# Constants built at the start, the last product on another engine, and the first expert's search work in another order, in an attention and two-layer expert kernel

## The chip, the cores and the metric

One core of a Trainium2 chip. The time is the device time of one launch, in microseconds (us); the kernel before has a median of 1419.82 us over three runs (1418.33 to 1420.47). The engines are TensorE (PE; its weight loads are listed as PEld), VectorE (DVE), ScalarE (ACT), GpSimd (POOL) and SyncE (SP, which only issues transfers here).

## The reference

Three stages, each fed by the one before.

```python
# attention with 32 state rows for each of 8 batches and 8 heads (S=512, D=64)
a  = softmax(x @ state.T / 8);  xread = a @ state
a2 = softmax(state @ x.T / 8);  sread = a2 @ x
x  = concat([xread, sread])                    # 4608 tokens x 512
# experts with a room of 576 tokens each: logits sorted over all (token, expert) pairs
for idx in argsort(-(x @ w_gate).flatten()):
    if token is free and expert has room: assign
for e in range(8): out[mask_e] = relu(x[mask_e] @ w1[e]) @ w2[e]
# gated layer on all tokens
out = (silu(out @ w_gate2) * (out @ w_val)) @ w_out
```

The assignment is a greedy walk through 36,864 sorted pairs. The kernel gets the same result by closing one expert after another: it finds which expert fills up first, at which threshold, gives that expert its tokens, and repeats.

## The kernel before, in words

**Attention** runs over the batches in a loop `for b in range(B + 1)`. A string names the order of the steps of one turn (`ORDER` for the middle turns, `HEAD` and `TAIL` for the first and the last): `z` the scores, `m` and `e` one softmax (`center`, `exps1`), `f` the other (`exps2`), `t` and `x` transposes, `r` and `s` the two products with the values (`xread`, `sread`), `p` and `q` the preparation of the next batch's state. Turn b finishes batch b-1 and starts batch b. `xread` leaves an undivided product `xu`; DVE takes the reciprocals `rd` of the sums, forms the router's logits (`xw`, summed into `Lw`), and POOL multiplies `xu` by `rd` into `xm`, which is stored in DRAM as `xm_d`. Step `c` builds constants for the search: in turn 1 the table `IE` on POOL, in turn 5 the rest of POOL's, in turn 6 those of DVE (lines 650 to 718). Step `k` in turn 7 makes the keys of the first 24 of 34 token columns and counts them (`keys`, `count128`, `digits`).

**The search** (`search`, `place`, `close`) works on one expert at a time. `keys` (lines 414 to 432) turns the best remaining logit of each token into an integer key and its digits. `count128` compares the top digit with 128 levels (tile `I`, DVE) and counts by matmuls with `G` (PE). Five more rounds refine the threshold: compare (`I`, DVE), count (PE), copy `ev`, sum (PE), `fe`, spread (PE), `jb`. `place` makes the list `idx` of the expert's token rows. `close` takes the expert out of the logits (`Lw`, line 595) and counts how much room every expert has left (`ca`, `cr`, `crb`, a matmul, `need`; lines 597 to 606).

**The experts** are 8 times 16 units: `hidden` makes 128 hidden columns for half of an expert's tokens (12 matmuls, tile `h`), `expert_out` multiplies them by the second weights (12 matmuls, tiles `y`). Weights and activations are split into an upper part (ACT) and a lower part (DVE: `lo[k]`, line 1014; `w`, lines 756 and 995; `xl`, line 813; `hl`, line 833). Tokens are fetched by `gather` (POOL, from `xm_d` by `idx`) and transposed by `turn` (PE into `bt`, ACT `xh`, DVE `xl`). A table `P_` says at which unit each load, gather, transpose and search is written: `lead` and `hook` for the search, `l0` and `lp` for 16 loads of 64-bit weights of the last layer, which are converted 6 units later. While the units of expert 0 run, the search for expert 1 runs between them on PE and DVE, since expert 1's tokens are not known before.

A list scheduler orders the instructions of each engine; each engine then runs its list in that order. `tc.issue_after(ins)` puts what follows behind `ins` on that instruction's own engine. What stands behind a waiting instruction on the same engine waits too.

After the experts the last layer fills PE with matmuls (line 1106) to the end.

Of the kernel before, what the change touches and what calls it, by code (L numbers as in the profile page):

```python
# [35 lines left out]
E = 8  # L36
# [9 lines left out]
P_ = {'spin': 20, 'xl': 2, 'pc': (0, 9), 'ct': 12, 'cuts': (0, 34), 'lead': [0, 1, 10, 25, 44, 57, 73, 89], 'hook': ['p', 'i', 'p', 'p', 'p', 'x', 'p', 'p'], 'w': [8, 14, 8, 8, 8, 8, 8, 8], 'whook': 'h', 'g': [0, 3, 18, 36, 56, 70, 85, 103], 'gs': 0.34, 't': [0, 14, 29, 46, 61, 75, 91, 104], 'ts': 1, 'ghook': 'p', 'thook': None, 't0': (2, 4, 5), 'l0': 10, 'lp': 6.2, 'cd': 6, 'lhook': 'hh', 'chook': 'h', 'swap': [], 'y0': 16, 'f0': [10, 4, 3]}  # L46
PRE = 24
HEAD = "z0 m0 f0 p l z1 m1 x0 x3 x2 e0 f1 x1 e1 q"
ORDER = "z0 f0 p t0 t1 z1 G l m0 f1 x0 m1 r0 x1 s0 e0 r1 x2 x3 r2 s1 k e1 c q r3"
# [8 lines left out]
def moe_kernel(ctx: ExitStack, tc: tile.TileContext, x, state, moe_w_gate, moe_w1, moe_w2,  # L58
# [57 lines left out]
    def load_state(b0, b1):  # L116
        for g in range(2):
            nc.scalar.dma_start(S2[:, b0:b1, g, 0, :],
                                state[b0:b1, 4 * g:4 * g + 4].rearrange("b h n d -> (h n) b d"))
        nc.gpsimd.tensor_copy(S2[:, b0:b1, :, 1, :], S2[:, b0:b1, :, 0, :])  # L120
        nc.gpsimd.tensor_copy(SC[:, b0:b1, :, :D], S2[:, b0:b1, :, 0, :])
# [19 lines left out]
    load_x(0)  # L141
    wg4 = ac.tile([64, H, E], F32, name="wg4")
# [83 lines left out]
    def turn_x(b, r):  # L226
# [6 lines left out]
        if True:  # L233
# [6 lines left out]
            nc.vector.tensor_tensor(xl[:, :, r, :], v, f32(xh[:, :, r, :]), OP.subtract)  # L240
# [66 lines left out]
    def xread(b, r):  # L307
# [10 lines left out]
        for g in range(2):  # L318
# [6 lines left out]
            nc.scalar.copy(xu[:, r % 2, 4 * g:4 * g + 4].rearrange("p h c -> p (h c)"), px)  # L325
        if r % 2:
# [9 lines left out]
            if b < B - 1 or r == 1:  # L336
                rm = aw.tile([128, 2, H], F32, name="rm", bufs=2)
                nc.vector.tensor_copy(rm, rd)
                rd = rm

            def values(rd=rd):
                hooks["m"] = nc.gpsimd.tensor_tensor(xm[:, q], xu[:, :, :, :D],
                                                     rd[:, :, :, None].to_broadcast([128, 2, H, D]), OP.mult).ins
# [3 lines left out]
            if b < B - 1 or r == 1:  # L347
                values()
            else:
                late.append((values, rd))  # L350
# [51 lines left out]
    def keys(c0, c1, first):  # L402
# [13 lines left out]
        if not first:  # L416
# [5 lines left out]
        nc.vector.tensor_tensor(t8, t8, w8b, OP.mult)  # L422
        sh, bits = DIGITS[0]
        nc.vector.tensor_scalar(dgi[:, 0], key, sh, (1 << bits) - 1,
                                op0=OP.logical_shift_right, op1=OP.bitwise_and)
        nc.vector.tensor_reduce(am, t8, AX.X, OP.max)
# [33 lines left out]
    def search(i, psum, partial=None):  # L460
        pieces = ((0, 6), (6, 9)) if i == 0 else tuple(zip(P_["pc"], P_["pc"][1:]))
# [42 lines left out]
    def place(i, psum, found):  # L504
# [63 lines left out]
        cuts = [0, 8, 16, 24, NC] if i == 0 else P_["cuts"]  # L568
# [12 lines left out]
    def close(i, psum):  # L581
# [13 lines left out]
        nc.vector.tensor_tensor(Lw, Lw, dn[:, None, :].to_broadcast([128, NC, E]), OP.add)  # L595
# [4 lines left out]
        hooks["cr"] = nc.vector.tensor_reduce(cr, ca.rearrange("p c e -> p e c"), AX.X, OP.add).ins  # L600
# [8 lines left out]
    IE = sel.tile([128, 129, 4], BF, name="IE")  # L609

# [4 lines left out]
    prep_gate(0)  # L615

    for b in range(B + 1):
        steps = ORDER if 0 < b < B else HEAD if b == 0 else TAIL
        for op in steps.split():
# [27 lines left out]
            elif k == "c":  # L647
                if b == 1:
                    with tc.issue_after(hooks["m"]):
                        nc.gpsimd.iota(IE, pattern=[[1, 129], [0, 4]], base=0, channel_multiplier=0,  # L650
                                       allow_small_or_imprecise_dtypes=True)
                elif b == 5:
                    with tc.issue_after(hooks["m"]):
                        I32i = ac.tile([128, 32, 4], BF, name="I32i")
                        nc.gpsimd.iota(I32i, pattern=[[1, 32], [0, 4]], base=1, channel_multiplier=0,
                                       allow_small_or_imprecise_dtypes=True)
                        units = sel.tile([128, 6], F32, name="units")
                        unit = sel.tile([128, 6, 128], BF, name="unit")
                        for s in range(6):
                            nc.gpsimd.memset(units[:, s:s + 1], 2.0 ** (-6 * s))  # L660
                            nc.gpsimd.memset(unit[:, s, :], 2.0 ** (-6 * s - (2 if s else 0)))

                        SL_i = ac.tile([128, 4, 4, 32], F32, name="SL_i")
                        nc.gpsimd.iota(SL_i, pattern=[[1, 4], [0, 4], [4, 32]], base=0, channel_multiplier=-1,
                                       allow_small_or_imprecise_dtypes=True)
                        onesf = ac.tile([128, 128], F32, name="onesf")
                        nc.gpsimd.memset(onesf, 1.0)
                        trif = ac.tile([128, 128], F32, name="trif")
                        nc.gpsimd.affine_select(trif, onesf, pattern=[[1, 128]], compare_op=OP.is_gt, fill=0.0,
                                                base=0, channel_multiplier=-1)  # L670
                        minus1 = sel.tile([128, 128], BF, name="minus1")
                        nc.gpsimd.memset(minus1, -2.0 ** -7)
                        ones2 = sel.tile([128, 2], BF, name="ones2")
# [724 lines left out]
```

## Time and profile before

| | |
|---|---|
| median of 3 runs | 1419.82 us |
| the profiled execution | 1420.64 us |
| its span, first to last instruction | 1418.1 us |
| PE busy | 1357.2 us, 96% |
| DVE busy | 1053.9 us, 74% |
| ACT busy | 571.7 us, 40% |
| POOL busy | 441.8 us, 31% |
| mean granted clock of TensorE | 0.98 |

The shares are means over stages that differ. Attention lasts to about 146 us, the first search to 171.6 us, the eight experts to about 620 us, and the last layer from there to the end. In the last two PE is the busy engine; ahead of them DVE is.

### The profile page before, as it was taken

The page shows a single profiled execution, that of the slowest core. Times are in us where ns is not written, and L with a number is a line of the kernel's source. Part 1 is how long each engine was busy: PE and PEld are TensorE (multiplying, and loading weights), DVE is VectorE, ACT ScalarE, POOL GpSimd, SP SyncE. Part 2 cuts the span into 40 slices and gives each one's busy share as a digit, 9 for nine tenths or more (in the row PEclk, how much of TensorE's full clock was granted, in tenths as well). Part 3 has the DMA queues.
Part 4 walks back from the last instruction along what each step waited for, and adds up shares of the span by engine and source line. Part 5 has one row for each costly group of instructions (what it writes and reads, how often), then busy time and mean ns, then how long its engine had stood idle before and what let it go on. Part 6 is the DMA issues. An engine that isn't in the chain of part 4 may idle for free.

```text
span 1418.1 us, 28991 instructions
## 1 busy us (share of the span) xinstructions
PE 1357.2 (96%) x11449; PEld 1318.0 (93%) x11449; DVE 1053.9 (74%) x2067; ACT 571.7 (40%) x1124; POOL 441.8 (31%) x388
## 2 busy tenths in 40 slices
PE   6998489999999999999999999999999999999996
PEld 5876288999999999999999999999999999999996
DVE  5879778886987664559767677776667788998872
ACT  6885123333333343434324335332333464444440
POOL 5766201010201010434213210012211108788871
PEclk9999599999999999999999999999999999999999
DMA  7542325543454454437547466455675784344431
GB/s 135 131 117 82 119 75 195 179 152 123 158 176 151 145 190 144 144 126 263 179 149 248 177 230 235 153 201 193 243 270 208 260 305 149 120 147 151 150 104 45
DMA packets 123335, 238.36 MB, mean 168 GB/s; under 512 B 47808, under 2 KB 57024, under 8 KB 116800
## 3 DMA queue, kind: packets, MB, share of 16 engines
q1 hardware_dynamic: 110096, 209.75, 43.8%
q0 software_dynamic: 5536, 17.83, 3.7%
q10 hardware_dynamic: 7568, 8.95, 2.1%
q8 instruction: 89, 1.46, 0.4%
q14 instruction: 46, 0.38, 0.1%
HBM read 153.65 MB, written 82.84 MB: 167 GB/s over the span
## 4 chain that ended last, share of the span: by engine, by line
PE 81%; DVE 6%; issue 5%; ACT 3%; DMA 2%; POOL 1%; ACTq 0%; POOLq 0%; SPq 0%; DVEq 0%
PE b L1106 50%; PE h L828 13%; PE y L847 4%; PE y L843 4%; PE y L844 4%; PE bt L807 1%; PE pt L236 1%; PE ps L363 1%; PE acc L483 1%; ACT xu L325 1%; ACT RBh L220 1%; DVE yb L872 1%; DMA xg<-xm_d,idx 1%; DMA raw<-y_d 0%; ACT zb L288 0%
## 5 line engine op out<-in xcount | busy, mean ns | idle before, releaser
L1106 PE MATMUL b<-yb,w 128*128 128x256 f32 x4320 | 516.2, 282 | 3.4 <-DVE cs L1156 2.5
L1106 PEld LDWEIGHTS b<-yb,w 128*128 128x128 f32 x4320 | 515.2, 190 | 4.3 <-DVE cs L1156 3.1
L1106 PE MATMUL b<-w,yb 128*128 128x256 f32 x2160 | 257.7, 282 | 0.0
L1106 PEld LDWEIGHTS b<-w,yb 128*128 128x128 f32 x2160 | 257.5, 189 | 0.0
L828 PE MATMUL h<-xh,w 128*128 128x288 f32 (+1 forms) x1024 | 209.7, 297 | 1.7 <-DVE hl L833 1.0
L828 PEld LDWEIGHTS h<-xh,w 128*128 128x128 f32 x1024 | 162.6, 190 | 3.4 <-DVE hl L833 1.7
L872 DVE TENSOR_TENSOR yb<-tt,yb 128x512 fp32r<-128x512 f32 x164 | 144.9, 897 | 21.7 <-ACT yb L871 20.9
L872 DVE TENSOR_TENSOR yb<-raw,yb 128x512 fp32r<-128x512 f32 x127 | 129.8, 1030 | 38.7 <-ACT yb L871 38.4
L798 POOL DMA_INDIRECT xg<-xm_d,idx x38 | 44.2, 1164 | 361.1 <-PE bt L807 158.9
L828 PE MATMUL h<-xl,w 128*128 128x288 f32 (+1 forms) x512 | 147.9, 291 | 0.7 <-DVE xl L813 0.7
L871 ACT CAST yb<-tt 128x512 fp32r<-128x512 f32 x164 | 100.2, 620 | 106.3 <-PE b L1106 70.6
L897 POOL TENSOR_TENSOR tt<-raw 128x512 f32<-128x512 f32 (+1 forms) x33 | 44.0, 1337 | 317.1 <-DMA raw<-m_d 129.4
L843 PE MATMUL y<-hh,w 128*128 128x288 f32 (+1 forms) x512 | 136.4, 292 | 1.2 <-ACT hh L832 1.2
L844 PE MATMUL y<-hh,w 128*128 128x288 f32 (+1 forms) x512 | 135.9, 291 | 0.0
L832 ACT ACTIVATE hh<-h 128x288 fp32r<-128x288 f32 (+1 forms) x128 | 50.6, 396 | 188.4 <-PE h L828 164.9
L833 DVE SCALAR_TENSOR_TENSOR hl<-h,hh 128x288 fp32r<-128x288 f32 (+1 forms) x128 | 55.9, 437 | 65.0 <-ACT hh L832 63.9
L871 ACT CAST yb<-raw 128x512 fp32r<-128x512 f32 x127 | 77.8, 620 | 57.8 <-PE b L1106 48.0
L843 PEld LDWEIGHTS y<-hh,w 128*128 128x128 f32 x512 | 97.2, 190 | 1.5 <-ACT hh L832 1.4
L828 PEld LDWEIGHTS h<-xl,w 128*128 128x128 f32 x512 | 96.5, 189 | 0.9 <-DVE xl L813 0.9
L844 PEld LDWEIGHTS y<-hh,w 128*128 128x128 f32 x512 | 97.1, 190 | 0.0
L847 PE MATMUL y<-hl,w 128*128 128x288 f32 (+1 forms) x512 | 89.8, 294 | 0.0
L847 PEld LDWEIGHTS y<-hl,w 128*128 128x128 f32 x512 | 74.1, 191 | 0.0
(261 smaller groups left out, 1999.1 us busy)
## 6 DMA issues: line engine op xcount, KB each, us to landing
raw<-in_moe_w_dram SPq DMA_DIRECT2D x64, 512.0 KB, 5.4
raw<-m_d SPq DMA_DIRECT2D x28, 1024.0 KB, 5.2
m_d<-m SPq DMA_DIRECT2D x48, 512.0 KB, 2.8
raw<-v_d SPq DMA_DIRECT2D x32, 512.0 KB, 5.4
raw<-y_d SPq DMA_DIRECT2D x14, 1024.0 KB, 4.8
xm_d<-xm SPq DMA_DIRECT2D x8, 1024.0 KB, 4.5
y_d<-ys SPq DMA_DIRECT2D x16, 512.0 KB, 6.7
sums_dy<-tt SPq DMA_DIRECT2D x32, 256.0 KB, 4.2
```

The lines of the kernel that those rows point to most:

```text
L220: nc.scalar.copy(rh[p, :, h, :], SC[p, b])
L798: hooks["g"] = nc.gpsimd.indirect_dma_start(out=xg[:n], out_offset=None, in_=xm_d, in_offset=bass.IndirectOffsetOnAxis(ap=idx[i][:n, j:j + ...
L828: hooks["p"] = nc.tensor.matmul(ph, W[i][0][k][q == 1][:, fs], (xl if q == 2 else xh)[:, k, :T], start=(n == 0), stop=(n == 11)).ins
L832: relu[16 * i + 8 * hf + f] = hooks["hh"] = nc.scalar.activation(hh, ph, AF.Relu).ins
L833: hooks["h"] = nc.vector.scalar_tensor_tensor(hl, ph, 0.0, f32(hh), op0=OP.max, op1=OP.subtract).ins
L843: nc.tensor.matmul(p[d], wh[:, f % 2, ds_], hh, start=(f == 0), stop=False)
L844: nc.tensor.matmul(p[d], wl[:, f % 2, ds_], hh, start=False, stop=False)
L847: nc.tensor.matmul(p[d], wh[:, f % 2, ds_], hl, start=False, stop=(f == 7))
L871: nc.scalar.copy(hi, src)
L872: nc.vector.tensor_tensor(lo, src, f32(hi), OP.subtract)
L897: nc.gpsimd.tensor_tensor(S1, a21, a22, OP.add)
L1106: nc.tensor.matmul(p[:, q], a(x, q), b(y), skip_group_check=True, start=start and not (q or n or m), stop=stop and q == 1 and n == last an ...
```

## The change

Constants: all of step `c` goes. POOL's 28 instructions are written behind the state copies of batch 0 and DVE's 17 behind the first four `xl` of batch 0.

On DVE, between the reciprocals of turn 6, these names were constants: `I32c`, `SL`, `tri`, `onesb`, `rq_i`, `rq` and six short fills. Before:

```order
L698 TENSOR_SCALAR SL<-SL_i 128x512
L374 TENSOR_TENSOR ss<-ps,rd_1578 32x128 x4
L700 CAST tri<-trif 128x128
L702 MEMSET onesb 128x128
L704 TENSOR_SCALAR rq_i<-rowid 128x34
L705 TENSOR_SCALAR rq_i<-rowid 128x34
L709 MEMSET A_1612 128x34
L711 MEMSET need 128x8
L707 CAST rq<-rq_i 128x68
```

Now, on DVE at the start of the kernel (`SBl` is the lower part of a batch's state, `zt` the first scores, `mx` and `nmx` their maxima):

```order
L691 MEMSET G 128x144
L694 MEMSET Dm_297 128x18
L694 MEMSET Dm_298 128x18
L303 STREAM_TRANSPOSE zt<-z_302 128x512
L317 TENSOR_REDUCE mx<-z_302 128x1
L305 TENSOR_REDUCE m_311<-zt 128x16
L318 TENSOR_SCALAR nmx<-mx 128x1
L245 TENSOR_TENSOR SBl_108<-pt,SBh_106 64x2x32 x4
L303 STREAM_TRANSPOSE zt<-z_339 128x512
```

The constants stand ahead of the first `zt`, and `SBl` of batch 1, which stood ahead of it, now stands behind `nmx`.

The end of attention: the products `xm` of the last batch are 32 activations on ACT with a scale per row, behind the last `xu`, in place of two multiplications on POOL; the copies of `rd` for them go. Step `k` is written behind `r3`.

The first expert: the four lower parts `lo[k]` stand behind the new `Lw`, without the room count ahead of them; the first eight instructions of `keys` follow; the room count (now `count_room`) stands behind the rest of `keys`. Searches 0 and 1 both cut their comparisons into pieces. Expert 1's lower first weights stand behind its index list. DVE behind index list 0, before:

```order
L595 TENSOR_TENSOR Lw<-Lw,dn 128x272
L597 TENSOR_TENSOR t_2287<-A_1612,e1io 128x272
L414 TENSOR_REDUCE V<-Lw 128x34
L600 TENSOR_REDUCE cr<-t_2287 128x8
L418 TENSOR_SCALAR un<-A_1612 128x34
L419 TENSOR_SCALAR sg<-V 128x34
L602 CAST crb<-cr 128x8
L420 TENSOR_TENSOR t_2378<-Lw,V 128x272
L605 TENSOR_SCALAR need<-acc 128x8
L421 TENSOR_TENSOR key<-V,sg 128x34
L1014 TENSOR_TENSOR w<-raw,w 128x1024
```

And now (line 1023 is the old line 1014):

```order
L644 TENSOR_TENSOR Lw<-Lw,dn 128x272
L1023 TENSOR_TENSOR w<-raw,w 128x1024 x4
L462 TENSOR_REDUCE V<-Lw 128x34
L466 TENSOR_SCALAR un<-A_289 128x34
L467 TENSOR_SCALAR sg<-V 128x34
L468 TENSOR_TENSOR t_2322<-Lw,V 128x272
L469 TENSOR_TENSOR key<-V,sg 128x34
L470 TENSOR_TENSOR t_2322<-t_2322,w_162 128x272
L472 TENSOR_SCALAR dgi<-key 128x34
```

The lower parts moved ahead of the wait for the room count's matmul (`need<-acc`).

The change of experts: the first two transposes of expert 1 are written between the last `expert_out` calls of expert 0 instead of at unit 15. DVE from index list 1 on, before (line 756 is expert 1's lower first weights):

```order
L756 TENSOR_TENSOR w<-raw,w 128x1024
L565 TENSOR_TENSOR rh<-T_2609,rq 128x34x6 x2
L756 TENSOR_TENSOR w<-raw,w 128x1024
L576 COPY dp<-acc 128x12
L855 COPY ys<-y_2733 128x256
L577 TENSOR_TENSOR dp<-dp 128x2x5
L855 COPY ys<-y_2735 128x256
L578 TENSOR_TENSOR idx_79<-dp 128x5
L756 TENSOR_TENSOR w<-raw,w 128x1024
L833 SCALAR_TENSOR_TENSOR hl<-h,hh 128x288
L756 TENSOR_TENSOR w<-raw,w 128x1024
```

And now (line 1065 is expert 1's lower first weights, line 654 the room count's sum):

```order
L627 TENSOR_TENSOR idx_79<-dp 128x5
L472 TENSOR_SCALAR dgi<-key 128x34
L635 TENSOR_TENSOR fit<-fit,sm 128x34
L487 TENSOR_SCALAR dgi<-key 128x34 x2
L636 TENSOR_TENSOR A_289<-A_289,fit 128x34
L487 TENSOR_SCALAR dgi<-key 128x34 x2
L651 TENSOR_TENSOR t_3056<-A_289,e1io 128x272
L1065 TENSOR_TENSOR w<-raw,w 128x1024 x4
L654 TENSOR_REDUCE cr<-t_3056 128x8
```

Two of the four lower parts stood ahead of the index list; now all four stand behind it and ahead of the room count. On PE at the same place (`bt` holds the first gathered tokens of expert 1), before:

```order
L843 MATMUL y_3336<-hh,w 128x288
L844 MATMUL y_3336<-hh,w 128x288
L807 MATMUL bt<-ident,xg 128x128 x3
L604 LDWEIGHTS onesb
L604 MATMUL acc<-crb,onesb 128x8
L828 MATMUL h<-xh,w 128x288 x2
L828 MATMUL h<-xl,w 128x288
```

And now (line 658 is the room count's matmul, line 507 the count of search 2):

```order
L848 MATMUL y_3368<-hh,w 128x288
L849 MATMUL y_3368<-hh,w 128x288
L812 MATMUL bt<-ident,xg 128x128 x3
L658 LDWEIGHTS onesb
L658 MATMUL acc<-crb,onesb 128x8
L812 MATMUL bt<-ident,xg 128x128
L507 LDWEIGHTS I
L507 MATMUL acc<-G,I 128x8
```

The next unit's matmuls (`h`) stood between the transposes and the count; now the count follows at once.

The core of the diff:

```diff
-P_ = {... 'hook': ['p', 'i', 'p', ...], ... 'l0': 10, 'lp': 6.2, ...}
+P_ = {... 'hook': ['p', 'x', 'p', ...], ... 'l0': 18, 'lp': 5.7, ...}
-ORDER = "... r2 s1 k e1 c q r3"
+ORDER = "... r2 s1 e1 q r3 k"
     load_state(0, 1)
     load_x(0)
+    with tc.issue_after(hooks["S", 0]):
+        nc.gpsimd.iota(IE, ...)
...
+    with tc.issue_after(hooks["xt"]):
+        for s in range(1, 6):
+            nc.vector.tensor_scalar(I32c[:, s - 1], I32i, 2.0 ** (-6 * s), None, op0=OP.mult)
...
-            if b < B - 1 or r == 1:
+            if b < B - 1:
                 rm = aw.tile([128, 2, H], F32, name="rm", bufs=2)
...
+                else:
+                    for j in range(2):
+                        for h in range(H):
+                            nc.scalar.activation(xm[:, r - 1 + j, h, :], xu[:, j, h, :D], AF.Copy,
+                                                 scale=rd[:, j, h:h + 1])
...
-        pieces = ((0, 6), (6, 9)) if i == 0 else tuple(zip(P_["pc"], P_["pc"][1:]))
+        pieces = ((0, 6), (6, 9)) if i < 2 else tuple(zip(P_["pc"], P_["pc"][1:]))
...
-    keys(PRE, NC, True)
-    with tc.issue_after(hooks["key"]):
-        for f, rd in late:
-            rd2 = aw.tile([128, 2, H], F32, name="rd", bufs=3)
-            nc.vector.tensor_copy(rd2, rd)
-            f(rd2)
+    list(keys(PRE, NC, True))
+    with tc.issue_after(hooks["xu"]):
+        for f in late:
+            f()
...
-    with tc.issue_after(hooks["cr"]):
+    with tc.issue_after(hooks["lw"]):
         for k in range(4):
-            nc.vector.tensor_tensor(lo[k], first[k], f32(hi[k]), OP.subtract)
+            hooks["lo"] = nc.vector.tensor_tensor(lo[k], first[k], f32(hi[k]), OP.subtract).ins
+    with tc.issue_after(hooks["lo"]):
+        key_parts = keys(0, NC, False)
+        next(key_parts)
...
+            if k == 1:
+                with tc.issue_after(hooks["key"]):
+                    count_room(bpsum)
             place(k, bpsum, search(k, bpsum))
...
     def first_of_two():
-        W[1] = ([], [])
-        load_w1(1, expert_id(1), nc.vector)
...
+        with tc.issue_after(hooks["i"]):
+            for k in range(4):
+                nc.vector.tensor_tensor(lo[k], raws[k], f32(hi[k]), OP.subtract)
...
+        if u == 16:
+            expert_out(*pend.pop(0))
+            for j in range(2):
+                turn(1, j)
+            expert_out(*pend.pop(0))
```

## Rows read from the trace of the kernel before

**Rows 1.** Maxima of the first half's scores, one a turn, DVE: start, length, instruction [idle before].

```profile
70.26 0.69 DVE L275 TENSOR_REDUCE mx<-z 128x1 f32<-128x512 f32 x1 [0.71 <-PE z L255]
...
84.51 0.69 DVE L275 TENSOR_REDUCE mx<-z 128x1 f32<-128x512 f32 x1 [0.65 <-PE z L255]
...
102.33 0.69 DVE L275 TENSOR_REDUCE mx<-z 128x1 f32<-128x512 f32 x1 [1.62 <-PE z L255]
...
120.96 0.69 DVE L275 TENSOR_REDUCE mx<-z 128x1 f32<-128x512 f32 x1
```

**Rows 2.** Stretches: busy us (instructions) of PE, PEld, DVE, ACT, POOL; clock, DMA.

```profile
87.50:104.90 17.40, 15.82 (x92) 13.82 (x91) 13.05 (x35) 12.88 (x37) 11.01 (x26) 0.90 0.41 102
...
113.90:121.00 7.10, 6.35 (x36) 5.38 (x37) 6.94 (x24) 5.51 (x17) 6.43 (x7) 1.00 0.04 9
121.00:129.00 8.00, 4.66 (x22) 3.35 (x22) 7.97 (x25) 4.35 (x12) 3.37 (x3) 0.94 0.32 133
...
230.00:240.00 10.00, 10.00 (x100) 9.84 (x99) 8.12 (x19) 2.36 (x4) 0.95 (x1) 0.83 0.19 63
...
300.00:400.00 100.00, 100.00 (x978) 97.30 (x978) 79.94 (x229) 33.65 (x63) 11.96 (x8) 1.00 0.49 164
```

**Rows 3.** The start, DVE and ACT, and POOL's first table.

```profile
16.20 0.93 DVE L203 TENSOR_TENSOR SBl<-pt,SBh 64x64 fp32r<-64x64 f32 x4 [2.73 <-ACT SBh L198]
17.50 0.72 DVE L261 STREAM_TRANSPOSE zt<-z 128x512 f32<-128x512 f32 x1 [0.37 <-PE z L255]
19.43 0.14 DVE L276 TENSOR_SCALAR nmx<-mx 128x1 f32<-128x1 f32 x1
...
19.48 1.07 ACT L239 CAST xTh<-pt 128x512 fp32r<-128x512 f32 x2 [1.96 <-PE pt L236]
...
41.13 1.21 POOL L650 IOTA IE<- 128x516 bf16 x1
```

**Rows 4.** DVE at the end of attention and in the first search, with POOL's two products.

```profile
135.04 0.49 DVE L438 TENSOR_SCALAR dgi<-key 128x24 int32<-128x24 int32 x5
...
141.76 0.18 DVE L329 TENSOR_SCALAR rd<-xu 128x16 f32<-128x16 f32 x1 [0.58 <-ACT xu L325]
...
143.37 1.34 DVE L329 TENSOR_SCALAR rd<-xu 128x16 f32<-128x16 f32 x1 [0.41 <-ACT xu L325]
...
148.16 2.05 DVE L438 TENSOR_SCALAR dgi<-key 128x10 int32<-128x10 int32 x3
...
142.76 1.92 POOL L342 TENSOR_TENSOR xm<-xu,rm 128x1024 f32<-128x1024 f32 x1 [3.29 <-ACT xu L325]
147.52 2.52 POOL L342 TENSOR_TENSOR xm<-xu,rd 128x1024 f32<-128x1024 f32 x1 [2.84 <-DVE rd L730]
```

**Rows 5.** ACT: small casts in attention, and the idle time behind attention.

```profile
102.77 0.87 ACT L198 CAST SBh<-pt 64x64 fp32r<-64x64 f32 x4
...
169.70 1.04 ACT L1006 CAST w<-raw 128x1024 fp32r<-128x1024 f32 x1 [26.19 <-DMA raw<-in_moe_w_dram]
```

**Rows 6.** The first units of expert 0, PE.

```profile
182.54 1.22 PE L828 MATMUL h<-xl,w 128*128 128x256 f32 x8 [0.69 <-DVE xl L813]
...
185.35 0.39 PE L843 MATMUL y<-hh,w 128*128 128x256 f32 x1 [1.16 <-ACT hh L832]
```

**Rows 7.** Around index list 1: DVE, POOL and PE.

```profile
221.59 0.15 DVE L578 TENSOR_TENSOR idx<-dp 128x5 int32<-128x5 f32 x1
...
223.16 1.21 DVE L756 TENSOR_TENSOR w<-raw,w 128x1024 fp32r<-128x1024 f32 x1
...
230.87 0.95 DVE L447 TENSOR_TENSOR I<-IE,Dm 128x1536 bf16<-128x1536 bf16 x1
...
222.49 1.23 POOL L798 DMA_INDIRECT xg<-xm_d,idx  x1 [43.85 <-issue]
...
229.74 0.55 PE L807 MATMUL bt<-ident,xg 128*128 128x128 f32 x3 [2.99 <-DMA xg<-xm_d,idx]
...
235.06 1.00 PE L458 MATMUL acc<-G,I 128*128 128x8 bf16 x34
```

More of the change, by code (lines that the diff above doesn't have):

```diff
@@ L567, in place @@
         ip = psum()[:, :2 * NK]
-        cuts = [0, 8, 16, 24, NC] if i == 0 else P_["cuts"]
+        cuts = [0, 8, 16, 24, NC] if i < 2 else P_["cuts"]
         for a, b in zip(cuts, cuts[1:]):
@@ L719, in moe_kernel @@
             elif k == "k" and b == B - 1:
-                keys(0, PRE, True)
+                list(keys(0, PRE, True))
                 part_p = ap.tile([128, 512], F32, name="pt", bufs=3)
@@ L993, in split_second @@
         raw = second.pop((i, k))
-        nc.scalar.copy(h, raw)
+        if i == 0 and k:
+            with tc.issue_after(hooks["hh"]):
+                nc.scalar.copy(h, raw)
+        else:
+            nc.scalar.copy(h, raw)
         nc.vector.tensor_tensor(l, raw, f32(h), OP.subtract)
@@ L1017, in moe_kernel @@
         spin(bp, "y2", 1, P_["spin"])
-    for j in range(2):
-        turn(0, j)
+    with tc.issue_after(hooks["kt"]):
+        for j in range(2):
+            turn(0, j)
     with tc.issue_after(hooks["g"]), tc.issue_after(hooks["xh"]):
@@ L1031, in select @@
         if k < E - 1:
-            keys(0, NC, False)
+            for _ in key_parts if k == 1 else keys(0, NC, False):
+                pass
+            if k == 1:
+                with tc.issue_after(hooks["key"]):
+                    count_room(bpsum)
             place(k, bpsum, search(k, bpsum))
@@ L1039, in first_of_two @@
     def first_of_two():
-        W[1] = ([], [])
-        load_w1(1, expert_id(1), nc.vector)
+        v = expert_id(1)
+        raws = [raw_w1(v, k) for k in range(4)]
+        hi = [wp.tile([128, F1], FR, name="w") for k in range(4)]
+        lo = [wp.tile([128, F1], FR, name="w") for k in range(4)]
+        for k in range(4):
+            nc.scalar.copy(hi[k], raws[k])
+        with tc.issue_after(hooks["i"]):
+            for k in range(4):
+                nc.vector.tensor_tensor(lo[k], raws[k], f32(hi[k]), OP.subtract)
+        W[1] = (list(zip(hi, lo)), [])
     at(2, "h", first_of_two)
@@ L1050, in moe_kernel @@
             at(P_["g"][k] + int(j * P_["gs"]), P_["ghook"], gather, k, j)
-            at(max(P_["t"][k] + j, 15 if k == 1 and j < 2 else 0), P_["thook"], turn, k, j)
+            if k > 1 or j > 1:
+                at(P_["t"][k] + j, P_["thook"], turn, k, j)
     for j in range(2, NT):
@@ L1068, in moe_kernel @@
                 fn(*args)
+        if u == 16:
+            expert_out(*pend.pop(0))
+            for j in range(2):
+                turn(1, j)
+            expert_out(*pend.pop(0))
         pend.append((i, hf, f) + hidden(i, hf, f))
```

165 lines of the change are left out of this document (81 added, 84 removed).

## The prediction

> **What bounds the kernel now.** I read the page first. PE is busy for 96% of the span, but that is a mean over stages, so I looked at stretches next. From 230 us on PE is full; 300 to 400 us stands for it, 100.00 of 100 us at the full clock [rows 2]. Nothing of the change but PE's own waits can move that part, so a gain has to come from the time ahead of it. There DVE is the busy engine: 6.94 of 7.10 us from 113.9 to 121, 7.97 of 8 up to 129 [rows 2]. A row a turn shows the pace of attention: the maxima of the first half start at 70.26, 84.51, 102.33 and 120.96 [rows 1]. A normal turn takes 14.25 us, turn 5 17.82, turn 6 18.63. Then I read DVE's waits and the instructions that are longer than their like, and at last the two places where PE waits in expert 0 and at the start of expert 1 [rows 6, 7].
>
> **A. The constants leave turn 6: -4.3 us.** DVE's 17 constants stand in turn 6, ahead of the row at 120.96, where DVE has no free time left. Without them I let the turn take what a normal one does: 18.63 - 14.25 = 4.4, taken as 4.3. The ends: nothing, if the turn is long for another reason, and 5.5, if turn 7 too finds PE and ACT less behind (the 6.94 us of DVE from 113.9 to 121 hold the constants almost whole). Turn 5 is just as long without any constant on DVE, and there the reason is another: PE's clock, 0.90 over it, and DVE is busy for 13.05 of 17.4 us only [rows 2]. That turn stays as it is. POOL's constants of turn 5 are counted with A, since POOL hands DVE the next tile.
>
> **B. The constants enter the start: +1.2 us.** DVE has a hole of 2.73 us ahead of the row at 16.20 [rows 3], and most of the 17 fit into it, since each is short when POOL doesn't hold it up. What moves with them is dearer: SBl of batch 1 (0.93 us) stood in that hole and now stands behind nmx, which ends at 19.57, so it ends near 20.5 instead of 17.13. Its PSUM buffer is one of three that the next transposes take in turn. In before the two xTh start at 19.48 [rows 3]; now the later of the transposes can only follow at about 20.7. That is 1.2 us, and I let it pass through, since a turn has the same length whenever it starts. The ends are 0 (a later wait covers it) and 2.4 (the same again for the instructions that POOL holds up, next).
>
> On POOL the constants stand between the state copies, 28 short instructions of which the longest is the table IE, 1.21 us [rows 3]. In this trace a DVE instruction beside a product on POOL ends when POOL's does: the reciprocal's first step at 143.37 takes 1.34 us instead of 0.18 and ends at 144.71, POOL's product at 144.68 [rows 4]. No row shows a fill or a table on POOL beside a DVE copy. [...]
>
> **C. The last batch: -1.8 us.** Its products xm go to ACT. POOL's product at 142.76 stretches DVE's step by 1.34 - 0.18 = 1.16 us [rows 4]; that goes. Step k behind r3 lets the list put e1l of the last batch ahead of two of the three comparison tiles, so DVE has that work left while PE and ACT make the last xu. The two waits for xu, 0.58 and 0.41 us [rows 4], are then covered: 0.99 us. What is late next: the key instructions that stood ahead of the second zb no longer cover POOL's zc for it, and DVE waits there, 0.4 us by my estimate. -1.16 - 0.99 + 0.4 = -1.75. The ends: -3.3, if no other instruction is held up by POOL in the new order either, and +0.4, if two more are (1.16 each).
>
> ACT pays nothing: 32 activations at 0.22 us, a quarter of the four casts of 64 columns [rows 5], are 7 us from about 143 us on, and ACT is idle for 26.19 us there [rows 5]. The store of xm then leaves at about 150 as before, 20 us ahead of the first gather. If that cover went, each us over 20 would be lost.
>
> **D. The first search: -1.6 us.** POOL's second product from 147.52 to 150.04 makes three digit steps on DVE take 2.05 us [rows 4]; five of them take 0.49 where POOL is free, so three take 0.3. They stand ahead of the sum that the search waits for: 1.75 us, of which 0.15 are then a wait for the count's matmuls. Nothing else in that chain changes. The ends: -1.75 and -0.8 (half of it hidden).
>
> **E. The first units of expert 0: +0.3 us.** The four lower parts no longer wait for the room count, and the second weights' casts no longer stand ahead of the first hh on ACT. PE's two waits, 0.69 for xl and 1.16 for hh [rows 6], go: -1.85. But the room count is now inside expert 0 and PE does the whole count of search 1 in one piece behind it: DVE must first finish G, the room count's two steps and the tiles I between two lower parts of 1.2 us. I work out 1.0 us of waiting ahead of the count, 0.6 behind it and 0.5 at the next transpose: +2.1. Ends -1.85 and +2.1. The load of a 64-bit weight moves from unit 10 to 18; PE is full in all the units where these loads and conversions fall [rows 2], so I price them at nothing.
>
> **F. The start of expert 1: +1.4 us.** Before: index list 1 ends at 221.74, the gather follows at 222.49, and PE waits 2.99 us for it until 229.74 [rows 7]. [...] Now PE has more matmuls ahead of the transposes. From index list 1 on I count 44 of them, at 0.13 us (eight take 1.22 with the tail of the last [rows 6]): 5.8 us. The gather is thereby covered, all but 2 us at its old length. But the count of search 2 stands right behind, and DVE comes to it late: from the list's end six small steps 1.2, four lower parts at 1.21 [rows 7] 4.8, the room count's sum 0.9, its matmul and need 0.4, four steps 0.9, three tiles I of up to 0.95 [rows 7] with G 3.1. That is 11.3, and the last matmuls make it 11.8. PE has 5.8 + 0.7 + 1.0 (the count, 1.00 [rows 7]) = 7.5 us of work in it, so it idles 4.3 us, against 2.99. [...]
>
> **The sum.** -4.3 + 1.2 - 1.8 - 1.6 + 0.3 + 1.4 = -4.8. The profiled execution took 1420.64 us, 2.5 more than its span; it becomes 1415.8. The median of the runs is 0.8 lower, and so the forecast for it is 1415.0.
>
> **The rivals.**
> 1. Turn 6 doesn't shrink. For it: turn 5 is as long and has no constants on DVE. Against: in turn 6 the clock is 1.00 from 113.9 to 121 and DVE is full [rows 2]. Then A is 0: 1419.3, no change.
> [...]
> 3. More is gained: C -3.3, B 0, E -1.0, F 0, with A and D as forecast, -10.2: 1409.6. For it: DVE is full in turn 7, so that every held-up instruction counts.
> 4. Slower: the lower parts of expert 1 become the bound at its start. Their weights are loaded after index 1's expert is known, and behind them on DVE stand the room count, the tiles I and hl, for which PE waits. Every us by which a load lands later than list 1 + 3 us is a us of PE's idle time, and it decides from 7.6 us on, where it has eaten the gain and 2.8 more. With 8 us: 1419.8 - 4.8 + 8 = 1423.0. For it: the four parts now stand in one piece. Against: before, a lower part runs at 223.16 [rows 7], 1.42 us behind the list's end at 221.74, so its load was there by then.
>
> **How the numbers follow.** A measurement of this kernel can tell 0.2%, 2.8 us, from no change: faster is below 1417.0, slower above 1422.7. The forecast (1411.5 to 1417) has 0.47, rival 3 0.13, rival 2 0.14, of which a quarter falls below 1417.0, rival 1 0.16, rival 4 0.10. Faster: 0.47 + 0.13 + 0.03 = 0.63. Slower: 0.10. Same: 0.27. The range for 8 in 10 runs from 1410.5, which leaves out half of rival 3, to 1420.5, which leaves out rival 4 and a little of rival 1; the likeliest case has 1411.5 to 1417.
>
> **What would show it.** A: the maxima of turns 6 and 7 lie about 14.3 us apart. B: the maxima of turn 1 start about 1.2 us later than now. C: the first step of rd in the last batch takes 0.18 us, with no wait for xu ahead of it. D: three digit steps take about 0.3 us. E: no wait for hh in the first units, one of about 1 us ahead of the count. F: PE idles about 4.3 us between the last unit's matmuls and the count of search 2, and no longer for the gather. The forecast is wrong if index list 0 ends less than 3 us earlier than at 171.6, or if PE's idle time at the start of expert 1 is over 8 us.

## The result and the profile after

The changed kernel takes 1430.45 us (median of 12 runs, 1426.2 to 1433.4); the kernel before took 1420.02 in the same comparison. The ratio is 1.007, 95% interval 1.0055 to 1.0084: 0.7% slower. The forecast was 1415.0, with a range up to 1420.5. The profiled execution of the changed kernel took 1427.07 us, with a span of 1425.4; it is one of the quicker ones, and the section on the experiments says why.

Most of what was forecast came, and was lost again at one place. The table takes the same instruction in both traces:

| point of the program | before, us | after, us | after minus before |
|---|---|---|---|
| maxima of turn 1, DVE | 28.92 | 30.39 | +1.5 |
| maxima of turn 6, DVE | 102.33 | 103.58 | +1.25 |
| maxima of turn 7, DVE | 120.96 | 117.09 | -3.9 |
| first keys of search 0 (V), DVE | 145.84 | 141.49 | -4.35 |
| index list 0, DVE | 171.41 | 165.33 | -6.1 |
| index list 1, DVE | 221.59 | 213.51 | -8.1 |
| 23rd ReLU of the experts (unit 22), ACT | 270.22 | 274.99 | +4.8 |
| end of the span | 1418.1 | 1425.4 | +7.3 |

Up to index list 1 the changed kernel leads by 8.1 us. A third of the way into expert 1 it is 4.8 behind. So 12.9 us went between 213 and 275 us, at the step called F. First the rows of DVE that answer to [rows 1, 3, 4], start, length, instruction and idle time before:

```profile
19.60 0.92 DVE L245 TENSOR_TENSOR SBl<-pt,SBh 64x64 fp32r<-64x64 f32 x4
...
103.58 0.69 DVE L317 TENSOR_REDUCE mx<-z 128x1 f32<-128x512 f32 x1 [1.70 <-PE z L297]
...
117.09 0.69 DVE L317 TENSOR_REDUCE mx<-z 128x1 f32<-128x512 f32 x1 [0.66 <-PE z L297]
...
138.17 0.18 DVE L371 TENSOR_SCALAR rd<-xu 128x16 f32<-128x16 f32 x1
...
139.39 0.17 DVE L371 TENSOR_SCALAR rd<-xu 128x16 f32<-128x16 f32 x1
...
140.67 0.17 DVE L440 COPY Lw<-pt 128x8 f32<-128x8 f32 x1 [0.82 <-PE pt L438]
...
143.73 0.31 DVE L487 TENSOR_SCALAR dgi<-key 128x10 int32<-128x10 int32 x3
```

Turn 6 lasts 13.5 us instead of 18.6, the two reciprocal steps of the last batch take 0.18 us and wait for nothing, and the three digit steps take 0.31 us instead of 2.05: the instructions of A, C and D changed as forecast. A new wait of 0.82 us stands ahead of the logits of the last rows.

Now the place where it went. DVE and POOL around index list 1, against [rows 7]:

```profile
213.51 0.16 DVE L627 TENSOR_TENSOR idx<-dp 128x5 int32<-128x5 f32 x1
...
214.22 0.44 DVE L651 TENSOR_TENSOR t<-A,e1io 128x272 f32<-128x272 f32 x1
214.58 4.62 DVE L1065 TENSOR_TENSOR w<-raw,w 128x1024 fp32r<-128x1024 f32 x4
...
228.41 0.17 DVE L659 TENSOR_SCALAR need<-acc 128x8 f32<-128x8 f32 x1 [8.02 <-PE acc L658]
```

```profile
214.42 5.62 POOL L803 DMA_INDIRECT xg<-xm_d,idx  x1 [39.92 <-PE h L833]
220.35 0.95 POOL L803 DMA_INDIRECT xg<-xm_d,idx  x1 [0.30 <-issue]
221.60 0.96 POOL L803 DMA_INDIRECT xg<-xm_d,idx  x1 [0.30 <-issue]
```

The first gather took 1.23 us before and takes 5.62 now. It begins 0.16 us ahead of the four lower parts and ends at 220.04, 0.84 us behind their end at 219.20. PE at the same time, and then the stretches (PE busy first, the clock third from the right):

```profile
227.44 0.90 PE L812 MATMUL bt<-ident,xg 128*128 128x128 f32 x3 [7.51 <-DMA xg<-xm_d,idx]
228.13 0.21 PE L658 MATMUL acc<-crb,onesb 128*128 128x8 bf16 x1
228.21 0.46 PE L812 MATMUL bt<-ident,xg 128*128 128x128 f32 x1
230.78 0.46 PE L507 MATMUL acc<-G,I 128*128 128x8 bf16 x12 [2.11 <-DVE G L481]
231.65 0.48 PE L507 MATMUL acc<-G,I 128*128 128x8 bf16 x12 [0.41 <-DVE I L496]
232.38 0.43 PE L507 MATMUL acc<-G,I 128*128 128x8 bf16 x10 [0.26 <-DVE I L496]
```

```profile
215.00:225.00 10.00, 4.93 (x38) 4.70 (x36) 5.39 (x9) 1.94 (x3) 6.95 (x3) 1.00 0.77 247
225.00:235.00 10.00, 4.51 (x47) 3.86 (x48) 6.05 (x16) 0.58 (x1) 0.95 (x1) 0.50 0.24 78
235.00:245.00 10.00, 10.00 (x83) 9.57 (x83) 6.14 (x16) 2.28 (x4) 0.00 (x0) 0.81 0.01 2
```

PE waits 7.51 us for a gathered piece, and not 2.99 as in [rows 7]. The matmul of the room count (L658) stands behind that wait, DVE's chain to the count of search 2 stands behind the room count, and so PE waits again for G and the tiles I. From 215 to 235 us it idles 10.6 us (20 - 4.93 - 4.51). From 225 to 235 us the granted clock is 0.50, and 0.81 in the next ten.

Which piece PE waits for is not in the trace, but in the order. The gathers of expert 1 on POOL fill xg_2753, xg_2755, xg_2757 in the kernel before, and xg_2787, xg_2789, xg_2791 after. The first transposes of expert 1 on PE, before (L807) and after (L812):

```
1271 L807 MATMUL bt_3465<-ident_70,xg_2753 128x128 x3
1271 L812 MATMUL bt_3528<-ident_70,xg_2791 128x128 x3
```

Before it was the first piece, now it is the third. The instructions read alike without the numbers. In the code the two turns of expert 1's first pieces moved into the block at unit 16, but the third piece's turn is in the plan of the same unit, and the plan is worked off ahead of the block.

The remaining 2.5 us of the end's +7.3 come later. PE's waits between 700 and 800 us, far behind every edit, make 2.4 of them (PE busy 96.72 of 100 us, before 99.09). These waits also differ among kernels that differ from the one before only near index list 1: PE is busy for 97.39 us there in hold_tt, 98.41 in hold_red and 98.45 in hold_gap (below). Their cause is not shown.

### The profile page after: what moved, and what is told of

Read it like the earlier page. It is cut to its first block, busy times and chain, and to the rows that moved or that the text cites. A ratio compares the mean times of both kernels' runs of the same rounds, so it can differ in the third digit from the quotient of the medians.

```text
span 1425.4 us, 29027 instructions
## 1 busy us (share of the span) xinstructions
PE 1357.2 (95%) x11449; PEld 1318.2 (92%) x11449; DVE 1052.9 (74%) x2073; ACT 579.2 (41%) x1156; POOL 442.5 (31%) x386
## 3 DMA queue, kind: packets, MB, share of 16 engines
q8 instruction: 90, 1.47, 0.4%
## 4 chain that ended last, share of the span: by engine, by line
PE 83%; DVE 5%; issue 5%; DMA 3%; ACT 3%; POOL 1%; SPq 0%; POOLq 0%; ACTq 0%; DVEq 0%
PE b L1137 51%; PE h L833 12%; PE y L852 4%; PE y L848 4%; PE y L849 4%; PE ps L411 1%; PE bt L812 1%; PE pt L278 1%; DMA xg<-xm_d,idx 1%; DMA raw<-in_moe_w_gate_dram 1%; PE acc L532 1%; DMA raw<-y_d 1%; ACT xu L367 1%; ACT RBh L262 0%; DMA xc<-in_x_dram 0%
## 5 line engine op out<-in xcount | busy, mean ns | idle before, releaser
L803 POOL DMA_INDIRECT xg<-xm_d,idx x38 | 48.2, 1267 | 376.6 <-PE bt L812 149.8
L1144 ACT ACTIVATE m<-b 128x256 f32<-128x256 f32 x60 | 22.8, 382 | 128.5 <-PE b L1137 125.1
```

The lines of the kernel that those rows point to most:

```text
L803: hooks["g"] = nc.gpsimd.indirect_dma_start(out=xg[:n], out_offset=None, in_=xm_d, in_offset=bass.IndirectOffsetOnAxis(ap=idx[i][:n, j:j + ...
L1144: hooks["silu"] = nc.scalar.activation(m, g, AF.Silu).ins
```

## The experiments

Theory H: the row of lower parts on DVE holds POOL's first gather up. Theory O: the loss comes from the order, PE stands at the third piece. Rival R: the gather is late by itself, or by the loads in flight. Twelve kernels were run. "Changed" is the kernel of the diff. The kernel before had a median of 1419.6 to 1420.4 us in each comparison.

**The attention half alone** (att_only: the constants, ORDER, the last batch on ACT; the expert edits left as in the kernel before).

> The kernel before with the attention half of the change alone (constants at the start, the order of the last turns, the last batch's products on ACT); expert 0 and expert 1 stay as they were. Theory 1: the 6.1 us that index list 0 gained in the changed kernel (165.4 us instead of 171.5) pass through to the end, since everything behind the list keeps its distance to it: 1420.0 - 6.1 = 1413.9 us, ratio 0.9957, and PE's wait for the first gathered piece of expert 1 stays near 3.0 us. Rival: a part of the gain is given back by the lower TensorE clock or by later loads, and less than 3 us remain: over 1417 us.

Measured 1414.51 us, ratio 0.9965 (0.9951 to 0.9979). PE's wait for the first piece is 3.0 us again. In this trace index list 0 comes at 166.24 us, 5.2 us earlier than before and not 6.1, and 5.1 us of that are in the medians: the gain passes through, and the rival falls.

**With expert 0's edits too** (e0_only: the changed kernel with the last three pieces of the diff undone):

```
-        hi = [...]; lo = [...]          # lower parts in one piece behind hooks["i"]
+        load_w1(1, expert_id(1), nc.vector)
-        if u == 16: expert_out(...); turn(1, 0); turn(1, 1); expert_out(...)
+        turn(1, 0), turn(1, 1) in the plan of unit 15
```

> The attention half together with the edits in expert 0 (the next search's keys, the room count inside the expert, the second weights' casts, the later loads of the 64-bit weights), while the start of expert 1 (its lower parts and the order of its first transposes) is as before. The forecast had +0.3 us for expert 0 on top of att_only (1414.5): 1414.8. The profiles bound it to between -2.6 and +1 us: 1412 to 1415.5. If the cost of the changed kernel sits in expert 0 after all, the time is over 1420. POOL's first gather should take 1.0 to 1.3 us.

Measured 1415.29 us, ratio 0.9965 (0.9951 to 0.9979). E is 0.8 us by the medians, and not to be told from nothing. So the new start of expert 1 costs 1430.45 - 1415.29 = 15.2 us.

**The third piece one unit later** (third_late):

```
-                at(P_["t"][k] + j, P_["thook"], turn, k, j)
+                at(P_["t"][k] + j + (k == 1), P_["thook"], turn, k, j)
```

> The changed kernel with one edit: the transposes of expert 1's third gathered piece stand one unit later in the code, so that PE comes to the first piece first, as in the kernel before. Theory H (POOL's first gather is held by the four lower parts on DVE for 4.4 us): the first piece still lands only about 6 us behind 220.0, so PE's wait shrinks from 7.5 us to about 6 and the kernel gains 1.5 to 2.5 us on the changed one (1430.4 to about 1428). Theory O (the loss is that PE waits for the third piece instead of the first): the wait goes back to about 3 us and 5 to 8 us are gained, 1423 to 1425 us.

Measured 1423.35 us, ratio 1.0029 (1.0017 to 1.004): 7.1 us better than the changed kernel. Its trace agrees with H on the wait, but the time is at O's end. POOL and PE:

```profile
217.95 5.63 POOL L803 DMA_INDIRECT xg<-xm_d,idx  x1 [42.95 <-PE h L833]
```

```profile
229.26 0.90 PE L812 MATMUL bt<-ident,xg 128*128 128x128 f32 x3 [6.16 <-DMA xg<-xm_d,idx]
```

The gather is held exactly as long again. PE's wait is 6.16 instead of 7.51, and from the 11th to the 23rd ReLU it takes 56.7 us instead of 60.9. So these two profiles show 4.2 of the 7.1 us; where the rest lies they do not show. They also show one thing that spreads the runs. The code is the same up to expert 0 and in it, yet the first ReLU comes at 181.52 us here and at 178.36 in the changed kernel: index list 0 is 0.5 us later here. The granted clock differs between executions too: from 172 to 180 us it is 1.00 in the changed kernel and 0.79 in e0_only, which has the same code there and its first ReLU at 180.00. Since some 3 us of this kind can lie between two executions, the medians decide.

**The lower parts elsewhere** (parts_back: each as soon as its weight is there, as before; parts_late: behind the keys and tiles of search 2):

```
 parts_back
-        with tc.issue_after(hooks["i"]):
-            for k in range(4): nc.vector.tensor_tensor(lo[k], raws[k], ...)
+        load_w1(1, expert_id(1), nc.vector)
 parts_late
-        with tc.issue_after(hooks["i"]):
+        with tc.issue_after(hooks["crb"]):        # emitted in unit 10
```

> The changed kernel with one part undone: expert 1's lower parts are made as before, each as soon as its weight is there (three of them ahead of index list 1), and not in one piece behind the list. Theory H: POOL's first gather takes 1.0 to 1.8 us instead of 5.6, and PE's idle time from 215 to 240 us falls from 10.5 to under 4 us; list 1 comes up to 2.4 us later; the sum is 7 to 10 us better than the changed kernel, 1420 to 1423 us, or better if the later list costs nothing. Rival R (the gather is late by itself or by the loads in flight, and the parts only stand beside it): the first gather keeps 4 us or more and the time stays over 1427 us.

> The changed kernel with expert 1's lower parts behind the room count and the keys of search 2 on DVE, and the second weights' loads of expert 1 behind them; the third piece's transposes are still the first on PE. Theory H: each of the three gathers takes about 1 us, the third piece lands near 222 us instead of 227.4, and PE's wait for it falls by about 5 us; the lower parts come 4 to 5 us later and cost at most 2 us of waiting ahead of expert 1's first unit: 1430.4 - 6 = about 1424 us. Rival R: the first gather takes 4 us or more without any lower part beside it. Theory O: PE still waits for the third piece, the wait is 5 us or more, and the time stays over 1427 us.

Measured 1416.03 (ratio 0.9972, 0.996 to 0.9983) and 1420.81 us (1.0005, 0.9992 to 1.0017), both faster than H had them. parts_late also has the loads of expert 1's second weights one unit later, which the lines above leave out. The first gather takes 1.22 and 1.12 us:

```profile
218.40 1.22 POOL L803 DMA_INDIRECT xg<-xm_d,idx  x1 [44.09 <-issue]
```

```profile
218.23 1.12 POOL L803 DMA_INDIRECT xg<-xm_d,idx  x1 [42.85 <-PE h L833]
```

R falls: the same gather, as idle before and with the same loads, is quick where no row of lower parts begins beside it. In parts_late PE does not wait for the third piece at all, but 3.9 us for a tile I that now stands behind the four lower parts, which is what is late next. Both kernels also have another order on PE, so they do not size H. They limit O, though: in parts_back the third piece still comes first in PE's order, but behind the count of search 2. PE uses it at 239.60 us without a wait, and e0_only, where the first piece comes first, is faster by 0.7 us only. So the third piece's place costs several us only where PE comes to it early.

**The two causes as a table of two** (parts_p1, and p1_third with the edit of third_late as well). The lower parts stand in one piece, one step later. The loads of expert 1's second weights also come one unit later (not shown in these lines), and the keys of search 2 are tied behind the lower parts:

```
         red = nc.vector.tensor_reduce(cr, ca..., AX.X, OP.add).ins
+        for l, r, h in pend_lo:           # the lower parts of expert 1
+            with tc.issue_after(red):
+                red = nc.vector.tensor_tensor(l, r, f32(h), OP.subtract).ins
-        nc.vector.tensor_copy(crb, cr)
+        with tc.issue_after(red):
+            nc.vector.tensor_copy(crb, cr)
```

> The changed kernel with two edits: expert 1's lower parts stand behind the room count's sum on DVE (about 0.5 us later than in the changed kernel, still in one piece and ahead of the keys of search 2), and the third piece's transposes one unit later. POOL's gather then has begun about 0.4 us ahead of the row. If that is enough for it to get its work done: 1.0 us, the first piece lands 7 to 8 us behind the list, PE waits 1 to 3 us, and the time is 1416 to 1419 us. If it waits for the end of the row again: over 5 us, and the time stays near that of third_late, 1423 us.

> p1_third without its second edit: expert 1's lower parts behind the room count's sum, the third piece's transposes first on PE again. It fills the table of two: lower parts where the changed kernel has them or one step later, third piece first or last. In p1_third the third gather ended on POOL at 220.5 us; by the 4.9 us from there to its use in the changed kernel it lands at about 225.4, and PE reaches the transposes at about 222: a wait of 3 to 4 us, and 1415 to 1417 us. If the third piece's place costs 7 us as between the changed kernel and third_late: 1419 us.

| median, us | third piece first | first piece first |
|---|---|---|
| lower parts behind t, as changed | 1430.45 | 1423.35 |
| lower parts behind cr | 1420.41 | 1411.81 |

The place of the lower parts is worth 10.0 and 11.5 us, the place of the third piece 7.1 and 8.6; together 18.6. parts_p1 missed the 1415 to 1417 us worked out from the gathers by 3.4 us, and is nearer to the 1419 of its other case: the third piece was in use only 6.3 us behind POOL's end (220.76 to 227.01), not 4.9, so PE waited 5.2 us. p1_third has the best median of the study, ratio 0.9947 (0.9928 to 0.9966) to the kernel before, better than I had expected. It is 3.5 us below e0_only: without the two faults the new start of expert 1 is a gain. No lower part stands ahead of index list 1 there, and the list's last step starts at 214.56 us, in e0_only at 217.56. POOL, DVE and PE of p1_third:

```profile
215.47 0.97 POOL L811 DMA_INDIRECT xg<-xm_d,idx  x1 [41.33 <-issue]
216.74 1.47 POOL L811 DMA_INDIRECT xg<-xm_d,idx  x1 [0.30 <-issue]
218.52 1.97 POOL L811 DMA_INDIRECT xg<-xm_d,idx  x1 [0.30 <-issue]
```

```profile
215.56 0.69 DVE L656 TENSOR_REDUCE cr<-t 128x8 f32<-128x272 f32 x1
216.17 4.62 DVE L659 TENSOR_TENSOR w<-raw,w 128x1024 fp32r<-128x1024 f32 x4
```

```profile
220.96 0.18 PE L666 MATMUL acc<-crb,onesb 128*128 128x8 bf16 x1
...
221.35 0.60 PE L820 MATMUL bt<-ident,xg 128*128 128x128 f32 x4
```

```profile
215.00:225.00 10.00, 9.47 (x77) 9.08 (x76) 9.93 (x25) 4.00 (x7) 5.36 (x4) 1.00 0.83 281
225.00:235.00 10.00, 9.90 (x110) 9.31 (x108) 8.88 (x24) 3.28 (x5) 0.00 (x0) 1.00 0.23 90
```

The row of parts is the same 4.62 us, 0.7 us after the gather's start instead of 0.16. The gather passes in 0.97 us, PE comes to the transposes when the piece is there, and idles 0.6 us from 215 to 235 instead of 10.6, at a granted clock of 1.00. From the 11th to the 23rd ReLU it takes 45.6 us, 15.3 less than in the changed kernel: 10.0 us of idle time, and about 4 of the clock, an estimate from PE's busy time and the granted clock of the two stretches in the changed kernel (4.51 us at 0.50 lose 2.3; 10 us at 0.81 lose 1.9).

**What it is in DVE's work that holds the gather** (one run each). Added to the kernel before, right behind index list 1, with results that nobody reads:

```
 hold_tt   for q in range(4): nc.vector.tensor_tensor(dummy, w_hi, w_lo, OP.subtract)
 hold_red  for q in range(4): nc.vector.tensor_reduce(dummy[:, q:q + 1], w_hi, AX.X, OP.max)
 hold_gap  one tensor_reduce over 890 columns, then the four of hold_tt
```

> The kernel before with four more subtractions on DVE right behind index list 1 (two fp32 operands of 128x1024 from SBUF, a result that nobody reads, the operands of the lower parts); two lower parts stand between them, so that about 6 us of such instructions follow each other. Theory H (an instruction on DVE with two operands in SBUF holds up POOL's gather, and the gather comes to its work when the row of them ends): the first gather takes 4 us or more instead of 1.23. Rival R (the gather was late by itself in the changed kernel): it takes 1.0 to 1.5 us as before.

> The same place and about the same length on DVE as in hold_tt, but each of the four added instructions is a maximum over one operand of 128x1024 in SBUF; two lower parts follow behind them. Theory H in its narrow form (two operands are what holds POOL up): the first gather takes 0.9 to 1.3 us, in the midst of DVE's work, and only a later one meets the two lower parts. Wide form (any work of DVE holds the gather up): the first gather takes 4 us or more, as in hold_tt.

> hold_tt with one more instruction, a maximum over 890 columns of one operand, ahead of the row of two-operand subtractions, so that the row begins about 0.15 us behind the start of POOL's first gather and not 0.8 us ahead of it. In hold_tt each gather that began inside the row waited for the end of the one instruction in progress (1.23, 1.95 and 1.97 us); in the changed kernel the gather began 0.16 us ahead of the row and took 5.62. Theory G (a gather that begins just ahead of such a row waits for the end of the row): the first gather takes 4 to 6.5 us here. Rival (the 5.62 have another reason, such as the loads that SP issues): it takes 1 to 2 us.

POOL's gathers in hold_tt, and POOL's and DVE's rows in hold_red and hold_gap:

```profile
221.79 1.23 POOL L798 DMA_INDIRECT xg<-xm_d,idx  x1 [42.83 <-issue]
223.32 1.95 POOL L798 DMA_INDIRECT xg<-xm_d,idx  x1 [0.30 <-issue]
225.58 1.97 POOL L798 DMA_INDIRECT xg<-xm_d,idx  x1 [0.30 <-issue]
```

```profile
222.53 0.97 POOL L798 DMA_INDIRECT xg<-xm_d,idx  x1 [42.98 <-issue]
```

```profile
221.69 4.59 DVE L1044 TENSOR_REDUCE dummy<-w 128x1 bf16<-128x1024 f32 x4
```

```profile
220.75 0.97 POOL L798 DMA_INDIRECT xg<-xm_d,idx  x1 [42.23 <-issue]
...
223.29 1.96 POOL L798 DMA_INDIRECT xg<-xm_d,idx  x1 [0.30 <-issue]
```

Beside the maxima over one operand no gather was held (0.97 us, and 0.95 for the next two); beside the subtractions of two operands all three of hold_tt were (1.23, 1.95 and 1.97 us). But two of my expectations failed. In hold_tt no gather waited for the row; each ended 0.83 to 0.85 us behind the one instruction that was in progress at its start. And in hold_gap the gather began 0.16 us ahead of the row, as in the changed kernel, and was not held. So theory G falls: the distance of 0.16 us does not decide by itself. The times of these three (1429.81, 1426.37 and 1419.33 us, one run each) hold DVE's added work as well.

**The 64-bit weights' loads at their old place** (back_l0 is parts_back, back_third_l0 has the edit of third_late too):

```
-'l0': 18, 'lp': 5.7
+'l0': 10, 'lp': 6.2
```

> The changed kernel with expert 1's lower parts made as before, and with the loads of the 64-bit weights started in unit 10 again (spacing 6.2) instead of unit 18 (5.7). The third piece's transposes are again the first on PE, early, with the room count's matmul between them, but no row of lower parts holds the gathers up. Theory O without H: PE waits 2 to 4 us for the third piece, 1417 to 1420 us. If the loads' move costs time by itself (2.4 us of PE's waits between 700 and 800 us in the changed kernel), that part goes and the time is 2 us lower than in parts_back otherwise: 1414 us.

> back_l0 with the third piece's transposes one unit later, so that the first piece comes first on PE. Against back_l0 it shows what the third piece's place costs where nothing holds the gathers up: by the distance of the gathers on POOL (1.25 us each) the wait is 2.5 us shorter, and the time 2 to 3 us lower; if the place costs as much as with the hold (7.1 us between the changed kernel and third_late), the time is 7 us lower.

Measured 1427.19 (ratio 1.0051, 1.0035 to 1.0066) and 1420.32 us (1.0006, 0.9994 to 1.0018). Inconclusive for what they were to tell: with the loads back, the order on PE and DVE around list 1 changes too, and the first gather took 3.44 us in the one and 0.97 in the other, so the 6.9 us between them hold H and O. back_l0 missed its 1417 to 1420 us by 7. No loss by the loads' move alone can be seen, but it is not ruled out: PE's waits between 700 and 800 us are 2.0 us in both, where the loads are at their old place, and 3.4 in parts_back and 1.6 in e0_only, where they have moved.

## Why the prediction was wrong

- **A, the constants leave turn 6 (-4.3): right, and 0.8 more.** The turn takes 13.5 us, 5.1 less; turn 5 stayed as long as it was, as forecast.
- **B, the start (+1.2): right in size.** SBl of batch 1 ends at 20.52, PE waits 1.78 us for what follows from it (sT), and the turns come 1.25 to 1.5 us later. The upper end, 2.4, did not come, and no run shows it as a price. But DVE's copies of the first x took longer beside POOL's table, which my sum left out. The four copies of the first x on DVE, before and after, with the table IE on POOL after:

```profile
6.86 1.43 DVE L106 COPY xc<-xc 128x512 f32<-128x512 f32 x4 [5.92 <-DMA xc<-in_x_dram]
```

```profile
7.10 2.59 DVE L106 COPY xc<-xc 128x512 f32<-128x512 f32 x4 [6.16 <-DMA xc<-in_x_dram]
```

```profile
6.85 1.20 POOL L144 IOTA IE<- 128x516 bf16 x1
21.19 0.66 PE L278 MATMUL pt<-ident,xc 128*128 128x128 f32 x4 [1.78 <-ACT sT L247]
```

  The longest copy takes 1.24 us beside the table, where each took 0.42 before. The four end 1.4 us later, but the first zt starts only 0.24 later (17.74 against 17.50): the waits between them took up the rest, and the sum was not hurt.
- **C, the last batch (-1.8): right in kind, 1.3 too large.** From the maxima of turn 7 to the keys the gain is 0.5 us (-4.35 against -3.9). Both waits and the stretched step went; the wait of 0.82 us for PE's logits is what came late next, and another 0.94 us for POOL's zc ahead of a transpose, where I had 0.4 in all.
- **D, the first search (-1.6): right.** -1.75.
- **The sum of these** was -6.5 and came as -6.1 at list 0; alone they make the kernel 5.1 us faster (att_only). That it came so near is in part luck, since A gave 0.8 more and C 1.3 less.
- **E, expert 0 (+0.3): right in number.** +0.8 by medians, within the spread. The waits for xl and hh went, and PE waits 0.90 us ahead of the room count's matmul, 0.64 ahead of the count and 0.34 at the next transpose, where I had 1.0, 0.6 and 0.5. A wait that I did not have came too: 1.87 us for the second gathered piece ahead of the first unit. What made up for it is not shown.
- **F, the start of expert 1 (+1.4): this step failed.** It measured +15.2 (changed against e0_only), and the sign that I had named, over 8 us of PE's idle time there, came with 10.6. I wrote that the gather "is thereby covered, all but 2 us at its old length" and put the count of search 2 behind DVE's work alone, with 4.3 us of idle time. Two assumptions in it were wrong. First, the gather did not keep its length: I priced the four lower parts as 4.8 us of DVE's time and did not ask what they do to POOL, although the gather begins right beside them. The table puts 10.0 to 11.5 us on this. Second, I took it that PE's first transposes are still the first piece's; without tile numbers the rows of the two pieces read alike. That is 7.1 to 8.6 us. Behind that wait the room count's matmul, which I had put 0.9 us behind the lower parts, came at 228.13, so DVE's chain ran after the wait and not beside it, and the clock stayed low for longer than before: 0.50 in every microsecond from 226 to 238, where the kernel before had it from 231 to 233. No run shows the term of 1.4 by itself: it was my estimate, 4.3 - 2.99 with a little on top and the clock's loss taken as equal; the runs showed 15.2 for the whole step.

  The warning stood in the trace of the kernel before. The gather at 222.49 in [rows 7] ends 0.85 us behind a lower part, and later a gather takes 2.72 us and ends 0.84 behind two comparisons in a row:

```profile
221.66 1.21 DVE L756 TENSOR_TENSOR w<-raw,w 128x1024 fp32r<-128x1024 f32 x1
...
381.77 1.81 DVE L447 TENSOR_TENSOR I<-IE,Dm 128x1536 bf16<-128x1536 bf16 x2
```

```profile
381.70 2.72 POOL L798 DMA_INDIRECT xg<-xm_d,idx  x1 [0.30 <-issue]
```

  And C and D rest on a hold between the same two engines, there of DVE beside POOL's products (1.34 us instead of 0.18, and 2.05 instead of 0.31). I weighed that and did not ask about the gather.
- **The rivals.** None had it. Rival 4 named the right instructions (expert 1's lower parts, in one piece) and almost the right sign and size, 1423.0, but by late loads. The parts run at 214.58 without a wait for a load, so its mechanism fell. I argued against it with the load alone. Rival 2 had its chance for a dearer start, and no run shows that: the turns came 1.25 to 1.5 us later.

## What to carry to other kernels

When instructions are moved on DVE, ask which gather of POOL begins beside them, and put long rows of two-operand instructions behind it; half a microsecond of place was worth 10 us here. Where a plan and the code order both place work, read the order with tile numbers: which piece PE stood at first was worth 7.1 to 8.6 us here. And count what stands behind a wait on each engine it feeds, since here a chain on DVE waited 8.02 us until PE's wait was over, and the granted clock was 0.50 from 225 to 235 us and 0.81 in the next ten.

## What the runs showed of the hardware

In these traces a gather on POOL that was held ended 0.82 to 0.87 us behind the end of the DVE instruction, or the row of instructions, that held it. Often that was the two-operand instruction in progress alone, 1.95 and 1.97 us in hold_tt, 1.47 and 1.97 in p1_third, and the gather then ran beside the next one. But some waited through the whole row that followed: four lower parts in the changed kernel and in third_late (5.62 and 5.63 us), two lower parts with two short instructions between and behind them in back_l0 (3.44 us), and rows of the search in other kernels, such as the 2.72 us of the kernel before. In hold_gap a gather that began at the same distance as in the changed kernel passed at once (0.97 us), and so did the first gather of expert 0 in the changed kernel itself, which begins with a row of four lower parts and takes 1.19 us:

```profile
166.46 4.65 DVE L1023 TENSOR_TENSOR w<-raw,w 128x1024 fp32r<-128x1024 f32 x4
```

```profile
166.45 1.19 POOL L803 DMA_INDIRECT xg<-xm_d,idx  x1 [30.68 <-DMA raw<-in_moe_w_dram]
```

The closest pair is back_l0 and back_third_l0. DVE has the same instructions around the gather's start in both, and the gather starts within 0.01 us of the same lower part. In back_l0 it is held, in back_third_l0 not, and there the lower part takes 0.03 us more:

```profile
221.44 3.44 POOL L803 DMA_INDIRECT xg<-xm_d,idx  x1 [46.30 <-issue]
221.45 1.22 DVE L761 TENSOR_TENSOR w<-raw,w 128x1024 fp32r<-128x1024 f32 x1
```

```profile
220.58 0.97 POOL L803 DMA_INDIRECT xg<-xm_d,idx  x1 [44.90 <-issue]
220.58 1.25 DVE L761 TENSOR_TENSOR w<-raw,w 128x1024 fp32r<-128x1024 f32 x1
```

So one trace of a kernel (0.97 us in back_third_l0) does not tell that a gather beside such a row is safe (3.44 in back_l0). In the two longest cases a short two-operand instruction (t, 214.22 in the changed kernel) was in progress at the gather's start and was followed without a gap; in hold_gap it was a maximum. That would fit, but hold_tt speaks against it as the whole rule: there too a two-operand instruction was in progress, followed by another. What decides is open.

The clock was the second surprise. In the changed kernel PE waits 7.51 us until 227.44, and its matmuls then run at a granted clock of 0.50 until 238 us. And where the code was the same, in expert 0 of e0_only and of the changed kernel, the clock was 0.79 in one and 1.00 in the other from 172 to 180 us, with the first ReLU 1.6 us apart.
